# A decode block on one core: w2's rows 16 to 19 loaded in three pieces by partitions, w2's transfer list recut, the output projection's weights in two transfers

## The chip, the cores and the metric

The kernel runs on one core of one Trainium2 chip. The metric is device time in microseconds (us) of one execution, the median of several runs. Before the change it is 139.92 us, the median of three runs from 139.88 to 140.01. One further execution was profiled; rows and durations in this text come from that one.

## The reference

Four sequences of one token each go through attention over a sliding window of a cache, and then through a gated feed-forward layer. Both parts have a layer norm ahead of them and a residual sum behind them. All arrays are bfloat16.

```python
def _A_ref(x, k_cache, v_cache, wq, wo):      # x: 4 x 1 x 1024
    W = min(4096, max(256, Sk // 4))          # Sk = 8192, so W = 2048
    q = (x @ wq).reshape(B, Sq, Hq, Dh).transpose(0, 2, 1, 3)     # 32 heads of 128
    k = jnp.repeat(k_cache[:, :, Sk - W:, :], rep, axis=1)        # 4 kv heads, each for 8 q heads
    v = jnp.repeat(v_cache[:, :, Sk - W:, :], rep, axis=1)
    p = softmax(jnp.einsum("bhqd,bhkd->bhqk", q, k) * Dh ** -0.5)
    o = jnp.einsum("bhqk,bhkd->bhqd", p, v)
    return o.transpose(0, 2, 1, 3).reshape(B, Sq, Hq * Dh) @ wo   # wo: 4096 x 1024

def _B_ref(x, w1, w3, w2):                    # w1, w3: 1024 x 3584; w2: 3584 x 1024
    return (silu(x @ w1) * (x @ w3)) @ w2

h = x + _A_ref(layernorm(x), k_cache, v_cache, wq, wo)
return h + _B_ref(layernorm(h), w1, w3, w2)
```

## The kernel before

There is little arithmetic and much to load: the windows of the two caches, and the five weight matrices, each byte of which is used once. The kernel is one straight program, and the order of instructions on each engine is the order in which they are written.

**The ring of loads.** Every large load goes through one list, `ring`, in the order k, wq, v, wo, w1, w3, w2. (Two of its entries, `kT`, load nothing: they are room for the transposed keys.) An entry takes one of five slots in SBUF, each of 128 partitions by 32 KB (`NSLOT`, `SLOT`). `fill()` walks the list. It issues the transfers of an entry from SP's queue at line 133, one per part of the entry, and it stops at an entry whose slot is not free. An entry's slot is free when every part of the entry five places earlier has been marked by `done()`, which calls `fill()` again. SP itself then waits until the readers of that slot have finished. All these transfers share SP's one hardware queue (q1 in the profile).

**wo.** `wo_v` puts 32 rows of `wo` on each partition, as four groups g (one for each kv head) of eight rows. Eight rows of 1024 bfloat16 numbers are 16 KB. `wo_` has four parts of one group each, 2 MB a transfer, and `pair` puts two of them into one entry. The loop at line 434 runs over g, then over eight rows t and four column blocks c. It reads `get("wo", g)` and calls `done("wo", g)` after each group. The slot of groups 0 and 1 is taken over by the second half of w3, and that of groups 2 and 3 by the first entry of w2.

**w2.** `w2_v` puts 28 rows of w2 on each partition, 2 KB each. `W2B = [16, 8, 2, 2]` cuts them into four transfers. The first, of 16 rows (4 MB), fills an entry by itself. The other three, of 8, 2 and 2 rows, share the last entry of the ring. Its slot comes free when the first half of w1 has been used. The loop at line 491 goes through the parts in order. For each row it has four matmuls, one per column block, with `hg_T` as the weights and 256 numbers of that row as the moving operand; 28 rows make 112 matmuls, accumulated in `y2_ps`. Then `res` adds the residual (line 501), and two small stores, on SP's and ACT's queues (lines 503 and 504), end the kernel.

**Order at the end.** PE goes through `y_ps` (wo), the second layer norm, `gu_ps` for w1 and then for w3, a transpose of the gated product by VectorE, and `y_ps` for w2. (The profile gives wo's and w2's accumulators the same name; the line tells them apart, 434 and 491.)

Of the kernel before, what the change touches and what calls it, by code (L numbers as in the profile page):

```python
# [17 lines left out]
NSLOT = 5  # L18
SLOT = 16384
NEG = -1.0e30  # L20


@with_exitstack
def kernel(
# [20 lines left out]
    nc = tc.nc  # L45

    B, _, D = A_x.shape
    Hkv, Sk, Dh = A_k_cache.shape[1], A_k_cache.shape[2], A_k_cache.shape[3]
# [11 lines left out]
    DQ = D // C  # L60
# [10 lines left out]
    T = REP  # L71
# [4 lines left out]
    wo_v = A_wo.rearrange("(g p t) n -> p g (t n)", g=Hkv, t=T)  # L76
# [16 lines left out]
    def pair(parts):  # L93
        return [parts[0:2], parts[2:4]]
# [3 lines left out]
        for name, cache in (("k", A_k_cache), ("v", A_v_cache))  # L98
    )
    kT_ = pair([("kT", b, [JR, P], None) for b in range(B)])  # L100
    wo_ = pair([("wo", g, [1, T * D], wo_v[:, g : g + 1, :]) for g in range(Hkv)])

    def four_rows(name, view, n):
        return [[(name, i, [4, n], view[:, 4 * i : 4 * i + 4, :])] for i in range(KC // 4)]

    wq_ = four_rows("wq", wq_v, NQ)
    ring = k_ + wq_[:1] + kT_ + wq_[1:] + v_ + wo_ + four_rows("w1", w1_v, F) + four_rows("w3", w3_v, F)
    W2B = [16, 8, 2, 2]
    w2_ = []
    f0 = 0  # L110
    for i, n in enumerate(W2B):
        w2_.append(("w2", i, [n, D], w2_v[:, f0 : f0 + n, :]))
# [6 lines left out]
    def fill():  # L119

        while len(taken) < len(ring):
            n = len(taken) - NSLOT
            if n >= 0 and not all((name, i) in used for name, i, _, _ in ring[n]):
                break
            parts = ring[len(taken)]
            slot = stream.tile([P, SLOT], BF16, tag="slot", name="s_" + parts[0][0])
            o = 0
            for name, i, shape, src in parts:
                dst = slot[:, o : o + int(np.prod(shape))]
                o += int(np.prod(shape))  # L130
                view = dst.rearrange("p (a b) -> p a b", a=shape[0])
                if src is not None:
                    nc.sync.dma_start(out=dst if name in ("k", "v") else view, in_=src)  # L133
                views[(name, i)] = view
            taken.append(slot)

    def get(name, i):
        return views[(name, i)]

    def done(name, i):  # L140
        used.add((name, i))
        fill()
# [5 lines left out]
    nc.vector.memset(x_nat[:], 0.0)  # L148
    nc.scalar.dma_start(out=x_nat[::S, :], in_=x_flat.rearrange("b (c n) -> c b n", c=C))
    fill()  # L150

    ident = const.tile([P, P], BF16)
# [8 lines left out]
        out=t32[:], in_=ident[:].rearrange("p (q h) -> p h q", q=C), axis=AX.X, op=ALU.add  # L161
# [4 lines left out]
    for q in range(C):  # L166
# [3 lines left out]
        out=negm[:], in_=t32[:].rearrange("p (g r) -> p g r", g=Hkv), axis=AX.X, op=ALU.add  # L170
    )
    nc.vector.tensor_scalar(
        out=negm[:], in0=negm[:], scalar1=-1.0, scalar2=-NEG, op0=ALU.add, op1=ALU.mult
    )
    jmask = const.tile([P, JM, 1], FP32)
    nc.vector.tensor_reduce(
        out=jmask[:, :, 0], in_=ident[:].rearrange("p (j h) -> p j h", j=JM), axis=AX.X, op=ALU.add
# [6 lines left out]
    for l in range(2):  # L184
        nc.gpsimd.tensor_copy(
            out=strip[:, l, B - 1 :].rearrange("p (c x) -> p c x", c=C)[:, :, : B * Hkv].rearrange(
                "p c (g b) -> p c g b", b=B
            )[:, :, :, 0],
            in_=t32[:].rearrange("p (g c l) -> p l c g", g=Hkv, c=C)[:, l],
# [62 lines left out]
    for i in range(KC // 4):  # L252
        w = get("wq", i)
        for kk in range(4):
            kc = 4 * i + kk
            for hf in range(2):
                for c in range(C):
                    o = (2 * c + hf) * HALF * Dh
# [3 lines left out]
                        rhs=w[:, kk, o : o + HALF * Dh],  # L262
# [15 lines left out]
    for b in range(B):  # L278
        nc.vector.tensor_copy(  # L279
            out=Qm[:, b].rearrange("p (g y) -> p g y", y=QW)[:, :, :REP],  # L280
            in_=qT_ps[:, :, :, S * b].rearrange("p r g -> p g r"),
# [125 lines left out]
    for l in range(2):  # L407
        for b in range(B):
# [3 lines left out]
                rhs=om[:, b],  # L412
# [10 lines left out]
        out=oP[:, :, :, ::S],  # L423
        in_=oX[:, :, : Hkv * B].rearrange("p t (g b) -> p g t b", b=B),
# [2 lines left out]

    y_ps = ps.tile([P, DQ], FP32, tag="kt0")
    for g in range(Hkv):
        w = get("wo", g)  # L430
        for t in range(T):
            for c in range(C):
                o = t * D + c * DQ
                nc.tensor.matmul(  # L434
                    y_ps[R * c : R * c + R, :],
                    lhsT=oP[:, g, t, :],
                    rhs=w[:, 0, o : o + DQ],
                    start=(g == 0 and t == 0),
                    stop=(g == Hkv - 1 and t == T - 1),
                    tile_position=(0, R * c),  # L440
                )
        done("wo", g)
    h1 = act.tile([P, DQ], FP32)
    nc.vector.tensor_tensor(out=h1[:], in0=y_ps[:], in1=x_nat[:], op=ALU.add)
    h_T = act.tile([P, KC, R], FP32)
# [40 lines left out]
    fc = 0  # L486
    for i, n in enumerate(W2B):
        w = get("w2", i)
        for ff in range(n):
            for c in range(C):  # L490
# [3 lines left out]
                    rhs=w[:, ff, c * DQ : (c + 1) * DQ],  # L494
# [40 lines left out]
```

## Time and profile before

| | |
|---|---|
| median of three runs | 139.92 us |
| the profiled execution | 140.13 us |
| its span, first to last instruction | 138.3 us |
| mean granted TensorE clock | 0.781 of full speed |
| busy: PE, PEld, DVE, ACT, POOL | 80.2, 47.5, 52.9, 42.7, 4.2 us |
| bytes read from HBM | 55.58 MB, 402 GB/s over the span |
| wo's transfers, 2 MB each: issue to landing | median 25.5 us, longest 29.9 us |
| w2's transfers: 16 rows; 8 rows; 2 rows (twice) | 28.0; 25.7; 27.0 us (median) from issue to landing |

PE is TensorE's matmuls, PEld its weight loads, DVE VectorE, ACT ScalarE, POOL GpSimd, and SP the engine that only issues transfers here. "L133" is line 133 of the kernel. A name such as `s_w` is a slot of the ring, with the buffer's number left out; `s_w` stands for w1, w3 and w2 alike. Engine rows are summed over the whole span; they overlap, so their sum is more than the span. In the page's row of 40 slices a digit is the busy share of a slice in tenths, with 9 for 90% or more. A chain of waits is followed backwards from the last instruction: at each step to whatever released it, or to the instruction ahead of it on its engine. The time of one execution is somewhat longer than its span, since it also holds what lies before the first instruction and behind the last.

### The profile page before, as it was taken

How to read it: one execution, taken by the hardware profiler on the slowest of the kernel's cores; microseconds unless marked ns; L12 is line 12 of the kernel's file. 1: busy time of each engine (PE TensorE's matmuls, PEld its weight loads, DVE VectorE, ACT ScalarE, POOL GpSimd, SP SyncE). 2: the span in 40 equal slices, each digit the busy share in tenths (PEclk: the TensorE clock that was granted, in tenths of full speed). 3: DMA queues.
4: the chain of work that ended last, by engine and by line, in shares of the span. 5: the costliest groups of instructions: out<-in, count | busy, mean ns of one | idle time of the engine just before them, and what ended most of it. 6: DMA issues, size and time to landing. Idle time of an engine off the chain costs nothing.

```text
span 138.3 us, 2012 instructions
## 1 busy us (share of the span) xinstructions
PE 80.2 (58%) x866; PEld 47.5 (34%) x868; DVE 52.9 (38%) x97; ACT 42.7 (31%) x57; POOL 4.2 (3%) x18
## 2 busy tenths in 40 slices
PE   0029898921903889328918998659539901703780
PEld 0029887820301322014304434537324400202550
DVE  3036676520000235177087197540330298350001
ACT  3005988850000325998807900000040200000000
POOL 7400000000000000000000000000000000000000
PEclk9999999998555799975797799965865896555555
DMA  4999999999989999999999999999999999999930
GB/s 152 399 423 431 431 436 455 455 441 398 445 384 426 441 417 417 450 407 431 450 400 431 433 469 431 394 448 448 419 398 448 456 411 430 445 407 398 406 148 2
DMA packets 3217, 55.72 MB, mean 403 GB/s; under 512 B 360, under 2 KB 392, under 8 KB 648
## 3 DMA queue, kind: packets, MB, share of 16 engines
q1 hardware_dynamic: 3178, 55.58, 94.4%
q8 instruction: 7, 0.11, 0.3%
q10 hardware_dynamic: 30, 0.01, 0.0%
q14 instruction: 2, 0.02, 0.0%
HBM read 55.58 MB, written 0.01 MB: 402 GB/s over the span
## 4 chain that ended last, share of the span: by engine, by line
DMA 49%; PE 27%; DVE 13%; ACT 4%; SPq 3%; issue 2%; DVEq 0%
DMA s_wq<-in_A_wq_dram 29%; DMA s_w<-in_B_w_dram 20%; PE o_ps L369 10%; PE y_ps L434 5%; ACT P L334 4%; PE sc_ps L294 3%; DVE PT L346 3%; SPq L133 3%; PE gu_ps L458 2%; PE q_ps L259 2%; DVE om L386 2%; DVE od L378 2%; PE on_ps L409 1%; PE tot_ps L355 1%; PE nm_ps L323 1%
## 5 line engine op out<-in xcount | busy, mean ns | idle before, releaser
L334 ACT ACTIVATE P<-sc_ps,bias 128x512 bf16<-128x512 f32 x16 | 19.7, 1417 | 9.6 <-DVE bias L331 9.6
L241 PE MATMUL kt_ps<-ident,s_k 128*128 128x128 bf16 x256 | 17.3, 228 | 1.3 <-ACT s_kT L245 1.0
L369 PE MATMUL o_ps<-s_v,PT 128*128 128x512 bf16 x62 | 17.5, 439 | 0.3 <-issue 0.2
L241 PEld LDWEIGHTS <-s_k 128*128 128x128 bf16 x256 | 16.3, 103 | 2.3 <-issue 1.7
L245 ACT COPY s_kT<-kt_ps 128x1024 bf16<-128x1024 bf16 x16 | 15.7, 1012 | 2.5 <-PE kt_ps L241 2.5
L458 PE MATMUL gu_ps<-s_w,n_T 128*32 128x448 bf16 x128 | 10.7, 513 | 8.8 <-DMA s_w<-in_B_w_dram 6.8
L259 PE MATMUL q_ps<-s_wq,n_T 128*32 128x512 bf16 x64 | 7.0, 615 | 11.8 <-DMA s_wq<-in_A_wq_dram 11.8
L243 DVE COPY s_kT<-kt_ps 128x1024 bf16<-128x1024 bf16 x16 | 11.1, 693 | 5.8 <-PE kt_ps L241 5.8
L491 PE MATMUL y_ps<-s_w,hg_T 128*32 128x256 bf16 x112 | 6.6, 418 | 8.0 <-DMA s_w<-in_B_w_dram 8.0
L369 PEld LDWEIGHTS <-PT 128*128 128x128 bf16 x64 | 7.2, 117 | 9.2 <-issue 4.4
L346 DVE STREAM_TRANSPOSE PT<-P 128x2048 bf16<-128x2048 bf16 x4 | 9.2, 2303 | 2.7 <-ACT P L334 2.7
L208 ACT ACTIVATE rstd<-rstd,eps_t 128x4 f32<-128x4 f32 x2 | 0.6, 297 | 29.5 <-DVE rstd L207 29.5
L458 PEld LDWEIGHTS <-n_T 128*32 128x32 bf16 x128 | 4.7, 131 | 14.1 <-issue 11.6
L294 PE MATMUL sc_ps<-s_kT,Qm 128*32 128x512 bf16 x64 | 8.5, 603 | 0.4 <-DVE Qm L279 0.4
L491 PEld LDWEIGHTS <-hg_T 128*32 128x32 bf16 x112 | 4.9, 142 | 10.0 <-issue 5.9
L259 PEld LDWEIGHTS <-n_T 128*32 128x32 bf16 x64 | 2.7, 137 | 15.6 <-issue 15.5
L269 DVE CAST q_sb<-q_ps 128x512 bf16<-128x512 f32 x1 | 0.7, 692 | 18.3 <-PE q_ps L259 18.3
L198 PE MATMUL sums_ps<-both,ones_f 128*128 128x64 f32 x4 | 1.1, 373 | 11.2 <-DVE both L196 11.2
L434 PE MATMUL y_ps<-s_wo,oP 128*32 128x256 bf16 x128 | 6.5, 397 | 1.7 <-DVE oP L422 1.7
L378 DVE SCALAR_TENSOR_TENSOR od<-o_ps,rinv,jmask 128x512 f32<-128x512 f32 x4 | 3.0, 751 | 8.4 <-PE o_ps L369 8.3
L270 ACT CAST q_sb<-q_ps 128x512 bf16<-128x512 f32 x1 | 0.6, 585 | 17.8 <-PE q_ps L259 17.8
L310 PE MATMUL mx_ps<-ident_f,rmax 128*1 128x128 f32 x8 | 1.7, 302 | 7.4 <-DVE rmax L308 7.4
(68 smaller groups left out, 64.7 us busy)
## 6 DMA issues: line engine op xcount, KB each, us to landing
s_w<-in_B_w_dram SPq DMA_DIRECT2D x4, 3584.0 KB, 21.2
s_k<-in_A_k_cache_dram SPq DMA_DIRECT2D x4, 2048.0 KB, 16.1
s_wq<-in_A_wq_dram SPq DMA_DIRECT2D x2, 4096.0 KB, 35.3
s_v<-in_A_v_cache_dram SPq DMA_DIRECT2D x4, 2048.0 KB, 25.1
s_wo<-in_A_wo_dram SPq DMA_DIRECT2D x4, 2048.0 KB, 25.5
s_w<-in_B_w_dram SPq DMA_DIRECT2D x1, 4096.0 KB, 28.0
s_w<-in_B_w_dram SPq DMA_DIRECT2D x1, 2048.0 KB, 25.7
s_w<-in_B_w_dram SPq DMA_DIRECT2D x2, 512.0 KB, 27.0
```

The lines of the kernel that those rows point to most:

```text
L241: nc.tensor.transpose(out=kt_ps[:, jj], in_=k[:, jb * JB + jj, :], identity=ident[:])
L243: nc.vector.tensor_copy(out=kT[:, jb * JB : (jb + 1) * JB], in_=kt_ps[:])
L245: nc.scalar.copy(out=kT[:, jb * JB : (jb + 1) * JB], in_=kt_ps[:])
L259: nc.tensor.matmul(q_ps[hf][R * c : R * c + R], lhsT=xn_T[:, kc, :], rhs=w[:, kk, o : o + HALF * Dh], start=(kc == 0), stop=(kc == KC - 1) ...
L294: nc.tensor.matmul(sc_ps[b][R * q : R * q + R], lhsT=Qm[:, b, g * R : (g + 1) * R], rhs=v[:, g, q], start=(g == 0), stop=(g == Hkv - 1), t ...
L334: nc.scalar.activation(out=P4[:, :, :, g], in_=sc_ps[b][:].rearrange("p (j i) -> p j i", i=L5), func=ACT.Exp, bias=bias[:, g : g + 1], sca ...
L346: nc.vector.transpose(out=PT[:].rearrange("p j h -> p (j h)"), in_=stage.pop(("P4", b))[:].rearrange("p j i g -> p (j i g)"),)
L369: nc.tensor.matmul(o_ps[:], lhsT=PT[:, i * JM : (i + 1) * JM, :].rearrange("p j h -> p (j h)"), rhs=v[:, i * JM : (i + 1) * JM, :], start= ...
L378: nc.vector.scalar_tensor_tensor(out=od[:], in0=o_ps[:], scalar=rinv[:, 0:1], in1=jmask[:].to_broadcast([P, JM, Dh]), op0=ALU.mult, op1=AL ...
L434: nc.tensor.matmul(y_ps[R * c : R * c + R, :], lhsT=oP[:, g, t, :], rhs=w[:, 0, o : o + DQ], start=(g == 0 and t == 0), stop=(g == Hkv - 1 ...
L458: nc.tensor.matmul(out_ps[hf][R * c : R * c + R], lhsT=hn_T[:, kc, :], rhs=w[:, kk, o : o + FH], start=(kc == 0), stop=(kc == KC - 1), til ...
L491: nc.tensor.matmul(y2_ps[R * c : R * c + R, :], lhsT=hg_T[:, fc, :], rhs=w[:, ff, c * DQ : (c + 1) * DQ], start=(fc == 0), stop=(fc == FC ...
```

## The change

It has three parts.

1. The four transfers of wo become two, each of two groups (4 MB). The projection's loop reads half of a transfer for each group, and marks a transfer as done after its second group.
2. w2 is cut into 16, 4, 4, 2 and 2 rows instead of 16, 8, 2 and 2. The last four parts share the last entry of the ring.
3. The second of these parts (rows 16 to 19 of each partition, 8 KB) is loaded by three transfers one after another on SP's queue, for partitions 0 to 111, 112 to 119 and 120 to 127.

The bytes loaded, the matmuls and their order are the same.

```diff
+PIECES = [0, 112, 120, 128]
...
-    wo_ = pair([("wo", g, [1, T * D], wo_v[:, g : g + 1, :]) for g in range(Hkv)])
+    wo_ = [[("wo", i, [2, T * D], wo_v[:, 2 * i : 2 * i + 2, :])] for i in range(Hkv // 2)]
...
-    W2B = [16, 8, 2, 2]
+    W2B = [16, 4, 4, 2, 2]
...
-                if src is not None:
+                if (name, i) == ("w2", 1):
+                    for p0, p1 in zip(PIECES[:-1], PIECES[1:]):
+                        nc.sync.dma_start(out=view[p0:p1], in_=src[p0:p1])
+                elif src is not None:
                     nc.sync.dma_start(out=dst if name in ("k", "v") else view, in_=src)
...
     for g in range(Hkv):
-        w = get("wo", g)
+        w = get("wo", g // 2)
...
-                    rhs=w[:, 0, o : o + DQ],
+                    rhs=w[:, g % 2, o : o + DQ],
...
-        done("wo", g)
+        if g % 2 == 1:
+            done("wo", g // 2)
```

## The prediction

> **What bounds the kernel now.** I read the page's DMA row first, then the chain of waits from its end, then the timeline of the last 30 us, then the last 3 us in quarter-microsecond windows.
>
> ```profile
> span 138.3 us, 2012 instructions
> DMA  4999999999989999999999999999999999999930
> q1 hardware_dynamic: 3178, 55.58, 94.4%
> ```
> The loads never pause: 55.58 MB go through SP's one queue, whose packets fill 94.4% of sixteen engines' span. The end of the chain of waits (start, length, what) says the same:
>
> ```profile
> 106.04 0.33 SPq L133
> 106.37 0.05 issue
> 106.42 0.43 SPq L133
> 106.84 0.05 issue
> 106.89 27.36 DMA s_w<-in_B_w_dram
> 134.26 0.04 issue
> 134.30 0.64 PE y_ps L491 x8
> 134.94 0.02 issue
> 134.97 0.42 DVE res L501
> ```
> The last w2 transfer is issued at 106.89 and lands 27.36 us later, because everything issued before it is ahead of it. After it come 0.64 us of matmuls, 0.42 us of `res` and the store. The timeline (start, length, engine, line) shows that PE has caught up by then:
>
> ```profile
> 126.88 3.61 PE L491 MATMUL y_ps<-s_w,hg_T 128*32 128x256 bf16 x64 [6.53 <-DMA s_w<-in_B_w_dram]
> ...
> 131.77 2.33 PE L491 MATMUL y_ps<-s_w,hg_T 128*32 128x256 bf16 x40 [1.28 <-DMA s_w<-in_B_w_dram]
> ...
> 134.30 0.62 PE L491 MATMUL y_ps<-s_w,hg_T 128*32 128x256 bf16 x8 [0.20 <-DMA s_w<-in_B_w_dram]
> ```
> So the last landing sets the time. The windows (stretch, its length, busy us of PE, PEld, DVE, ACT, POOL, clock, DMA share, GB/s) show that the sixteen engines do not finish together:
>
> ```profile
> 131.50:131.75 0.25, 0.00 (x0) 0.00 (x0) 0.00 (x0) 0.00 (x0) 0.00 (x0) 0.50 1.02 410
> 131.75:132.00 0.25, 0.23 (x8) 0.20 (x11) 0.00 (x0) 0.00 (x0) 0.00 (x0) 0.50 0.66 262
> 132.00:132.25 0.25, 0.25 (x12) 0.22 (x8) 0.00 (x0) 0.00 (x0) 0.00 (x0) 0.50 0.57 229
> 132.50:132.75 0.25, 0.25 (x12) 0.22 (x8) 0.00 (x0) 0.00 (x0) 0.00 (x0) 0.50 0.44 180
> 133.50:133.75 0.25, 0.25 (x12) 0.22 (x5) 0.00 (x0) 0.00 (x0) 0.00 (x0) 0.50 0.21 82
> 133.75:134.00 0.25, 0.25 (x8) 0.05 (x1) 0.00 (x0) 0.00 (x0) 0.00 (x0) 0.50 0.00 0
> ```
> At 131.75 all are busy; by 132.5 the share is 0.44, seven of sixteen; by 133.8 none.
>
> The trace's DMA records say which. Each packet has a start, a length and a size, but no engine; yet a packet starts 3 to 4 ns before the one ahead of it on its engine ends, so the records can be strung into sixteen chains. Each chain comes out as 176 data packets and 22 completion packets in SP's order. Their last w2 packets end at: seven between 131.73 and 132.00, then 132.31, 132.61, 133.07, and six between 133.62 and 133.78. The six late chains are those that also carried one of the six 16 KB instruction packets of queue q8 that start between 20.5 and 112.9 us; each put its chain back by some 1.7 us. The chain ending at 133.07 and that at 132.61 carried q14's two packets. The four chains that carried `x_nat` (sixteen rows on ACT's queue) are none of the six. Those four belong to eight chains that ran in step in the first 5 us; all six late ones come from the other eight, which then ran out of step. (For three of the six that half is less sure: between 46 and 80 us an end of theirs falls within 1 ns of one of the first eight's, where strings can be swapped.)
>
> **The change, part by part.** *wo in two transfers.* Two of four SP issues go (0.33 to 0.54 us each). The last wo transfer is issued at 53.2 and the longest takes 29.9 us to land: 83.1. PE's first read is at 92.28 and waits for DVE's `oP`. The slack is 9 us, the bytes are the same, and `fill()` acts after the same groups as before, since a slot is freed only when both its halves are used. Cost 0; without that slack a late landing would move `y_ps` one for one.
>
> *w2 as 16, 4, 4, 2, 2.* SP issues six transfers at the end instead of three: 6 x 0.43 = 2.6 us from 106.04, so to 108.6. Queue q1 still holds over 20 us of work then, which hides it (2.6 - 1.28 = 1.3 us if it did not); behind them on SP is only the store, at 135.42. PE's first matmul on the split part waits for three landings, not one. No row shows a triple wait; a queue step on the chain costs 0.02 to 0.14 us, so two more are 0.04 to 0.28 us. They fall where PE has room: the late chains get through that part some 4.9 us (2.44 + 1.22 + 1.22, for the eight rows behind it) before their end, at 128.6, and PE is on the first 64 matmuls until 130.49. Sixteen matmuls then take 16 x 58 ns (2.33 us for 40) = 0.93 us against 2.44 us between landings, and the last 8 still take 0.64. Nothing is added at the end.
>
> *The three pieces.* Four rows are 8 KB a partition. A 16 KB packet takes 0.609 us start to start, so 8 KB takes 0.305, and 64 KB (eight partitions) 2.44. With 112 partitions over sixteen engines each gets seven packets; the two pieces of eight partitions give, if eight engines share them, two more to these. So eight engines carry 9 x 8 KB and eight carry 7 x 8 KB where all carried 8: +0.305 us and -0.305 us. Completion packets (6 ns each) don't count. If the six late chains lie among the relieved eight, they end at 133.78 - 0.305 = 133.47, and the latest of the loaded eight at 133.07 + 0.305 = 133.38. The last data packet then comes 0.305 us earlier, and landing, matmuls, `res` and store follow as before.
>
> The trace only half supports that placement: few-row transfers do use few engines (`x_nat` four chains, the ACT store two), none of them late, and the six are in one half. [...]
>
> What no row shows is whether eight rows into neighbouring partitions, or 112 dealt by sevens, go at full pace. Lower bound: 0.305 us a piece; in `x_nat`, 512 B packets that overlap on two chains take 27 ns, as those alone do. Upper bound: all eight rows in turn, 2.44 us a piece, 4.88 for both where 0.61 is planned: +4.27 us on the loaded chains, whose latest would end at 137.65, 3.9 us past today's end. I take the lower, by the `x_nat` packets, and keep the upper for the range.
>
> [...]
>
> *Sum.* Profiled run: span 138.3 - 0.3 = 138.0, plus the 1.83 us around it (140.13 - 138.3) is 139.83. That run is 0.21 us over the median of 139.92, so the forecast is **139.62 us**.
>
> **Rivals.**
> 1. *The rows of a piece share one way in.* Four in turn, halfway in powers of two from one to eight, make a piece 1.22 us, and the loaded chains lose 2 x (1.22 - 0.305) = 1.83 us. The usual early chain ends at 132.0 + 0.305 + 1.83 = 134.1, 0.35 us late; the one at 133.38 ends at 135.2, 1.43 us late, if it meets others at all, being 1.1 us behind them. That is 140.27 to 141.35, about 140.8. It decides from where a piece costs 0.2 us more than planned: 133.38 + 2 x 0.2 is today's end. For it: eight adjacent partitions and engines that start together. Against: the early chains have 1.7 us to spare.
> 2. *A late chain is among the loaded eight.* Then 133.78 + 0.305: 140.22. Against: the halves above.
> 3. *The load spreads otherwise* (the pieces on all engines alike): 139.92, nothing changes.
> 4. *The next instruction packet.* It starts at 133.48, when PE is at about matmul 93 of 112, on an engine already idle for 0.4 us or more. Row 23 now lands 2.44 us before the late chains' end plus the 0.48 us from last packet to landing (133.78 to 134.26), at 131.5; 13 matmuls on, at 132.3, PE asks for that packet, 1.2 us sooner, and it could meet q1 packets: 1.1 us more on a chain that is last, 141.0. Against: the idle engine was not one of the six, so its relieved or early end leaves room.
>
> **How the numbers follow.** A measurement tells 0.2%, 0.28 us, from no change. Forecast case: 0.50, of which faster 0.32 and within 0.18 (0.305 us is hardly above 0.28). Rival 1: 0.32, slower 0.29, within 0.03. Rival 2: 0.07, slower 0.06, within 0.01. Rival 3: 0.04. Rival 4: 0.05, slower. The last 0.02 is for a larger gain. Faster 0.34, within 0.26, slower 0.40. The forecast's own range is 139.50 to 139.80; the whole reaches to rival 1's far end: 139.5 to 141.3, leaving out about one in ten for longer pieces.
>
> **What would show it.** Right: the last `y_ps` group starts near 134.0; late chains 0.3 us earlier and chains with `x_nat` 0.3 us later; `wo` landed before 84; DMA share at 132.5 above 0.44 and zero by 133.5. Rival 1: 8 KB packets of 0.5 us or more just before 131, with the `x_nat` chains last. Rival 2: the six late ones at 134.1. Rival 4: a q8 packet that overlaps w2 packets on a chain that ends last. I am wrong if the split part lands later than PE's 64th matmul, or if w2's rate falls below 400 GB/s before 131.

## The result, and the profile after

The changed kernel takes 144.08 us, the median of five runs from 143.94 to 144.34. The kernel before took 139.99 us beside it (five runs, 139.88 to 140.01). The ratio is 1.0296, with a 95% interval from 1.0282 to 1.0309. The change makes the kernel slower by 4.1 us; the forecast was 139.62, in a range from 139.5 to 141.3.

The profiled execution took 143.94 us. From its page, the span and the DMA rows, in 40 slices of 3.55 us:

```profile
span 142.1 us, 2013 instructions
...
DMA  4999999999999999999999999999999999999940
GB/s 148 427 415 434 424 438 489 443 411 406 424 406 429 438 434 411 420 429 438 436 424 411 454 453 412 433 436 420 433 428 428 452 429 415 406 242 189 344 180 2
```

The DMA engines are as busy as before, but from the 36th slice on they move 242, 189 and 344 GB/s, where mostly 400 to 450 is usual. A busy share says that packets are in flight; only the rate beside it says how fast. The end of the chain of waits (start, length, what) has the same form as before; line numbers are those of the changed kernel, whose L497 and L507 are L491 and L501 of the kernel before:

```profile
110.37 27.53 DMA s_w<-in_B_w_dram
137.91 0.04 issue
137.95 0.64 PE y_ps L497 x7
138.59 0.02 issue
138.62 0.42 DVE res L507
```

The last landing is still what PE waits for. It comes at 137.91 instead of 134.26, and these 3.65 us are nearly all of the difference between the two spans (142.1 - 138.3 = 3.8). To see where they arise, take the tail in windows of 2 us (stretch, length, busy us of PE, PEld, DVE, ACT and POOL, granted clock, DMA share, GB/s). First the kernel before, then the changed one:

```profile
124.00:126.00 2.00, 0.00 (x0) 0.00 (x0) 0.00 (x0) 0.00 (x0) 0.00 (x0) 0.50 0.77 328
126.00:128.00 2.00, 1.12 (x24) 0.98 (x27) 0.00 (x0) 0.00 (x0) 0.00 (x0) 0.50 0.96 410
128.00:130.00 2.00, 2.00 (x44) 1.75 (x40) 0.00 (x0) 0.00 (x0) 0.00 (x0) 0.50 1.02 432
130.00:132.00 2.00, 0.71 (x20) 0.35 (x13) 0.00 (x0) 0.00 (x0) 0.00 (x0) 0.50 0.91 367
```

```profile
124.00:126.00 2.00, 0.00 (x0) 0.00 (x0) 0.00 (x0) 0.00 (x0) 0.00 (x0) 0.50 0.96 254
126.00:128.00 2.00, 0.00 (x0) 0.00 (x0) 0.00 (x0) 0.00 (x0) 0.00 (x0) 0.50 0.90 193
128.00:130.00 2.00, 1.80 (x36) 1.53 (x39) 0.00 (x0) 0.00 (x0) 0.00 (x0) 0.50 1.06 176
130.00:132.00 2.00, 1.55 (x36) 1.06 (x28) 0.00 (x0) 0.00 (x0) 0.00 (x0) 0.71 0.96 221
132.00:134.00 2.00, 0.62 (x16) 0.45 (x17) 0.00 (x0) 0.00 (x0) 0.00 (x0) 1.00 0.94 350
```

Between 126 and 132 all sixteen engines together move 176 to 221 GB/s, half of what they did, and yet their share is 0.90 to 1.06. The clock of TensorE is no part of this; PE waits. In the DMA records, with their one duration per packet, 193 of the 256 packets of 8 KB take over 0.34 us (the usual one takes 0.31), the longest 1.11. Only 128 of the 256 belong to the pieces, so at least 65 packets of the four-row transfer behind them are slow too. Packets of the 16-row transfer *ahead* of the pieces are hit as well: on engines that are still at it, their 32 KB packets take up to 2.2 us instead of 1.22. From 133 on packets have their usual length again, and the last three transfers land 1.25 us apart, as transfers of 32 KB an engine at full pace do. Summed over all of w2's packets and divided by sixteen, the excess is 3.9 us an engine, which is the whole loss.

On PE one sees the same (timeline: start, length, engine, line, the idle time before it):

```profile
128.20 3.35 PE L497 MATMUL y_ps<-s_w,hg_T 128*32 128x256 bf16 x64 [8.40 <-DMA s_w<-in_B_w_dram]
133.20 0.62 PE L497 MATMUL y_ps<-s_w,hg_T 128*32 128x256 bf16 x16 [1.65 <-DMA s_w<-in_B_w_dram]
135.46 1.05 PE L497 MATMUL y_ps<-s_w,hg_T 128*32 128x256 bf16 x16 [1.64 <-DMA s_w<-in_B_w_dram]
136.71 0.62 PE L497 MATMUL y_ps<-s_w,hg_T 128*32 128x256 bf16 x8 [0.21 <-DMA s_w<-in_B_w_dram]
137.95 0.62 PE L497 MATMUL y_ps<-s_w,hg_T 128*32 128x256 bf16 x8 [0.62 <-DMA s_w<-in_B_w_dram]
```

The first 64 matmuls, on the transfer ahead of the pieces, already start 1.3 us later than before (126.88), and the split part is ready 1.65 us after they are done, at 133.20, where the forecast had PE still at work when it came. That, and a rate of some 200 GB/s before 131, are the two signs that the prediction named for being wrong.

### The profile page after: what moved, and what is told of

It is laid out like the page before. It is cut to its first block, busy times and chain, and to the rows that moved or that the text cites. A ratio compares the mean times of both kernels' runs of the same rounds, so it can differ in the third digit from the quotient of the medians.

```text
span 142.1 us, 2013 instructions
## 1 busy us (share of the span) xinstructions
PE 83.2 (59%) x866; PEld 49.1 (35%) x868; DVE 52.8 (37%) x97; ACT 42.8 (30%) x57; POOL 4.2 (3%) x18
## 4 chain that ended last, share of the span: by engine, by line
DMA 47%; PE 28%; DVE 13%; ACT 4%; SPq 3%; issue 2%; DVEq 0%
DMA s_wq<-in_A_wq_dram 28%; DMA s_w<-in_B_w_dram 19%; PE o_ps L374 10%; PE y_ps L439 5%; ACT P L339 4%; PE sc_ps L299 3%; DVE PT L351 3%; SPq L138 3%; PE gu_ps L464 2%; PE q_ps L264 2%; DVE om L391 2%; DVE od L383 2%; PE tot_ps L360 1%; PE nm_ps L328 1%; PE on_ps L414 1%
## 5 line engine op out<-in xcount | busy, mean ns | idle before, releaser
L246 PE MATMUL kt_ps<-ident,s_k 128*128 128x128 bf16 x256 | 18.4, 237 | 0.9
L374 PE MATMUL o_ps<-s_v,PT 128*128 128x512 bf16 x62 | 18.7, 463 | 0.3 <-issue 0.2
L246 PEld LDWEIGHTS <-s_k 128*128 128x128 bf16 x256 | 17.5, 109 | 1.8 <-issue 1.6
L464 PE MATMUL gu_ps<-s_w,n_T 128*32 128x448 bf16 x128 | 10.2, 496 | 6.4 <-DMA s_w<-in_B_w_dram 4.5
L497 PE MATMUL y_ps<-s_w,hg_T 128*32 128x256 bf16 x112 | 6.3, 383 | 12.5 <-DMA s_w<-in_B_w_dram 12.5
L497 PEld LDWEIGHTS <-hg_T 128*32 128x32 bf16 x112 | 4.2, 128 | 14.9 <-issue 8.9
L507 DVE TENSOR_TENSOR res<-y_ps,h 128x256 bf16<-128x256 f32 x1 | 0.4, 424 | 16.2 <-PE y_ps L497 16.2
```

Source lines behind the costliest of these rows:

```text
L246: nc.tensor.transpose(out=kt_ps[:, jj], in_=k[:, jb * JB + jj, :], identity=ident[:])
L374: nc.tensor.matmul(o_ps[:], lhsT=PT[:, i * JM : (i + 1) * JM, :].rearrange("p j h -> p (j h)"), rhs=v[:, i * JM : (i + 1) * JM, :], start= ...
L464: nc.tensor.matmul(out_ps[hf][R * c : R * c + R], lhsT=hn_T[:, kc, :], rhs=w[:, kk, o : o + FH], start=(kc == 0), stop=(kc == KC - 1), til ...
L497: nc.tensor.matmul(y2_ps[R * c : R * c + R, :], lhsT=hg_T[:, fc, :], rhs=w[:, ff, c * DQ : (c + 1) * DQ], start=(fc == 0), stop=(fc == FC ...
```

## The experiments

The theory after this reading, called P, was a supposition of the author's: a packet is slow while another engine writes to the same small group of partitions, which the pieces bring about and transfers of 128 partitions do not. The DMA records name neither the engine nor the partitions of a packet, so no run shows this itself; the runs show which pieces are slow, and by how much. Rivals were the recut itself, the eight-row pieces alone, reads from memory, and a cost that exists only at the tail.

**The change without its pieces**

```diff
-PIECES = [0, 112, 120, 128]
+PIECES = [0, 128]
```

> The change without its pieces: wo in two transfers and w2 as 16, 4, 4, 2, 2 stay, the four rows are one transfer of 128 partitions. Theory P (the pieces cost it all: packets that reach partitions in another way than 16 engines by eights slow each other): 139.7 to 140.2 us, the same as before, and the 8 KB packets take 0.31 us. Rival R (smaller packets and two more transfers in the queue, or the wo merge, cost part): 141 us or more with whole transfers too.

Measured: 139.90 us against 140.09 before, ratio 0.9992 (0.9983 to 1.0002). Its windows:

```profile
126.00:128.00 2.00, 1.18 (x24) 1.03 (x27) 0.00 (x0) 0.00 (x0) 0.00 (x0) 0.50 1.02 426
128.00:130.00 2.00, 2.00 (x47) 1.70 (x41) 0.00 (x0) 0.00 (x0) 0.00 (x0) 0.50 1.01 418
```

The rate stays at 418 to 426 GB/s with packets of 8 KB, all between 0.309 and 0.322 us. The wo merge and the recut cost nothing; the pieces cost all of it. This is the base for what follows.

**112 and 16 partitions**

```diff
-PIECES = [0, 112, 120, 128]
+PIECES = [0, 112, 128]
```

> The four rows in two pieces, 112 and 16 partitions. Theory P1 (the 112 piece, dealt by sevens, is most of the cost: in the changed kernel it took 3.9 us between its landing and the one before where seven packets need 2.1): 142 to 144 us. Rival Q (the two pieces of eight partitions, on eight engines, are the cost): 140 to 140.5 us, since neither is there.

Measured: 143.95 us, ratio 1.028 (1.026 to 1.0301), as slow as the change. Eight-row pieces are not needed for the loss.

**The 112 piece by itself**, beside whole transfers. In this and the later runs with repeated rows, the last slot's unused quarter takes rows a second time, and nothing reads them. Here `ROWS = [slice(0, 112)]`:

```diff
                 if (name, i) == ("w2", 1):
-                    for p0, p1 in zip(PIECES[:-1], PIECES[1:]):
-                        nc.sync.dma_start(out=view[p0:p1], in_=src[p0:p1])
+                    nc.sync.dma_start(out=view, in_=src)
+                    spare = slot[:, 12 * D : 16 * D].rearrange("p (a b) -> p a b", a=4)
+                    for rows in ROWS:
+                        nc.sync.dma_start(out=spare[rows], in_=src[rows])
```

> Whole transfers, and behind the four-row one a transfer that repeats partitions 0 to 111 into the unused part of the slot: the 112 piece by itself. It adds seven packets of 8 KB on each engine, 2.1 us at full pace: 142.0 us if the 112 piece runs at full pace (rival Q, the eight-partition pieces alone are slow). Theory P: its packets take 0.5 us or more and slow those of late engines: 143 to 145 us.

Measured: 145.44 us, ratio 1.0385 (1.0344 to 1.0426): 5.5 us over the base, where 2.1 would be full pace. The 112 piece is slow on its own, and takes 3.4 us too much. The rate, in windows of this run:

```profile
128.00:130.00 2.00, 2.00 (x48) 1.72 (x37) 0.00 (x0) 0.00 (x0) 0.00 (x0) 0.50 0.98 221
130.00:132.00 2.00, 1.10 (x24) 0.57 (x17) 0.00 (x0) 0.00 (x0) 0.00 (x0) 0.76 1.05 242
132.00:134.00 2.00, 0.00 (x0) 0.00 (x0) 0.00 (x0) 0.00 (x0) 0.00 (x0) 1.00 0.97 225
```

**The two pieces of eight adjacent partitions by themselves** (`ROWS = [slice(112, 120), slice(120, 128)]`)

> Whole transfers, and behind the four-row one two more transfers of eight adjacent partitions each (112 to 119, 120 to 127), which repeat part of its load into an unused part of the slot: 16 KB more on each of eight engines, 0.61 us if at full pace. Rival Q (pieces of eight adjacent partitions slow each other and their neighbours): 140.8 to 142 us. P1 (only the 112 piece hurts): 139.9 to 140.2, as the engines that carry them have 0.7 us or more to spare.

Measured: 142.12 us, ratio 1.0149 (1.0129 to 1.0169), 2.2 us over the base for 128 KB.

**The same pieces with partitions spread** (`ROWS = [slice(0, 32, 4), slice(32, 64, 4)]`)

> As the run with adjacent partitions, but the two repeated pieces hold partitions 0, 4, .. 28 and 32, 36, .. 60. The same bytes on the same number of engines. If nearness of the partitions is what slows a piece: 139.8 to 140.2 us here and clearly more with adjacent ones. If any transfer on eight engines costs the same: equal times in both.

Measured: 140.39 us, ratio 1.0026 (1.0014 to 1.0038), 0.5 us over the base, a little more than expected. The same bytes on as many engines; only the partitions differ. Windows with the adjacent pieces, then with the spread ones:

```profile
126.00:128.00 2.00, 1.26 (x25) 1.05 (x28) 0.00 (x0) 0.00 (x0) 0.00 (x0) 0.50 1.13 324
128.00:130.00 2.00, 2.00 (x45) 1.69 (x37) 0.00 (x0) 0.00 (x0) 0.00 (x0) 0.50 0.96 238
```

```profile
126.00:128.00 2.00, 1.12 (x24) 0.94 (x27) 0.00 (x0) 0.00 (x0) 0.00 (x0) 0.50 0.98 410
128.00:130.00 2.00, 2.00 (x44) 1.69 (x40) 0.00 (x0) 0.00 (x0) 0.00 (x0) 0.50 1.00 416
```

238 GB/s against 416. Of the 8 KB packets, the longest is 0.92 us with adjacent partitions and 0.32 with spread ones. Eight rows can go at full pace, and do so here, with the partitions four apart.

**Reads or writes**: the pieces' sources and destinations taken apart. First the adjacent rows of w2 into spread partitions, then the spread rows into adjacent partitions (`for to, of in ROWS: ... dma_start(out=spare[to], in_=src[of])`).

> The two repeated pieces with source and destination taken apart: they read the adjacent rows (those of partitions 112 to 127) and write them to partitions 0, 4, .. 60. [...] Rival U (reading adjacent rows of w2 from memory on several engines at once is slow): as with adjacent pieces, 141.8 to 142.4.

> The counterpart: the pieces read the rows of partitions 0, 4, .. 60 and write them to the adjacent partitions 112 to 127. Theory P: 141.8 to 142.4 us with 8 KB packets of up to 0.9 us. Rival U: 140.2 to 140.6.

Measured: 140.20 us, ratio 1.0012 (0.9999 to 1.0025), and 142.19, ratio 1.0148 (1.0119 to 1.0178). For these pieces the partitions written decide; which rows are read does not matter. The 112 piece and the halves of 64 were not taken apart in this way.

**Two halves of 64**

```diff
-PIECES = [0, 112, 120, 128]
+PIECES = [0, 64, 128]
```

> The change with the four rows in two halves of 64 partitions, sixteen engines each with four packets. [...] Rival T (dealing by sevens, with a size that is no power of two, is the trouble): 139.8 to 140.3.

Measured: 144.54 us, ratio 1.0321 (1.0245 to 1.0396). Powers of two are no better than sevens, so rival T is out. The median of the 8 KB packets is 0.59 us, nearly twice 0.31, and the time is 4.5 us over before. Four packets an engine for each half, at 0.59 instead of 0.31, are an estimate of 8 x 0.28 = 2.2 us. In the windows:

```profile
126.00:128.00 2.00, 0.00 (x0) 0.00 (x0) 0.00 (x0) 0.00 (x0) 0.00 (x0) 0.50 0.80 147
128.00:130.00 2.00, 1.30 (x28) 1.13 (x31) 0.00 (x0) 0.00 (x0) 0.00 (x0) 0.50 1.03 217
130.00:132.00 2.00, 2.00 (x44) 1.60 (x36) 0.00 (x0) 0.00 (x0) 0.00 (x0) 0.50 1.00 221
```

217 and 221 are half the usual rate. The estimate of 2.2 us leaves out two things. While some engines are already at the halves, 32 KB packets of those still at the transfer before take up to 2.5 us. And 194 of the 256 packets of 8 KB take over 0.34 us, though only 128 belong to the halves, so at least 66 of the transfer behind are slow as well. At 220 GB/s the 1 MB of the halves is an estimate of 4.8 us, yet the rate is down in all of these 6 us; what accounts for the rest, no run shows.

**Spread, but in the other half** (`ROWS = [slice(64, 96, 4), slice(96, 128, 4)]`)

> [...] Rival S (only crowding of neighbouring partitions counts, where an engine writes does not): as with the low spread pieces, 140.2 to 140.5, all packets 0.31 us.

Measured: 141.70 us, ratio 1.0118 (1.0086 to 1.015). So it isn't only crowding within the piece (rival S): these pieces are spread as widely as the low ones, 1.8 us over the base instead of 0.5. Packets go up to 0.63 us, and 116 of them are over 0.34 us, though the two pieces hold only sixteen. What sets these partitions apart from 0, 4, .. 60, no run shows.

**Spread, shifted by four partitions** (`ROWS = [slice(4, 36, 4)]`, one piece)

> [...]

Measured: 140.52 us, ratio 1.0034 (1.0023 to 1.0045). That is 0.6 us over the base for one piece, where two low spread pieces cost 0.5. 91 packets of 264 take over 0.34 us, the longest 0.54, though the piece holds only eight: neighbours are disturbed. In windows of 1 us:

```profile
126.00:127.00 1.00, 0.14 (x4) 0.13 (x7) 0.00 (x0) 0.00 (x0) 0.00 (x0) 0.50 1.02 426
127.00:128.00 1.00, 1.00 (x24) 0.83 (x20) 0.00 (x0) 0.00 (x0) 0.00 (x0) 0.50 1.04 328
128.00:129.00 1.00, 1.00 (x28) 0.83 (x24) 0.00 (x0) 0.00 (x0) 0.00 (x0) 0.50 0.99 352
129.00:130.00 1.00, 1.00 (x24) 0.85 (x20) 0.00 (x0) 0.00 (x0) 0.00 (x0) 0.50 0.94 352
130.00:131.00 1.00, 1.00 (x28) 0.85 (x17) 0.00 (x0) 0.00 (x0) 0.00 (x0) 0.50 1.02 418
```

A piece of 0.3 us lowers the rate for some 2.5 us. The disturbance outlasts the piece; why is open.

**The pieces in the middle of the stream**

```diff
-                if (name, i) == ("w2", 1):
+                if (name, i) == ("w3", 0):
```

> The pieces moved from the tail to the middle of the stream: w2's four rows whole, but the first half of w3 (four rows of 7 KB on each partition, 3.5 times the bytes) in pieces of 112, 8 and 8 partitions. Theory P (a piece loses bandwidth wherever it stands, in proportion to its bytes): the 4.1 us of the change times 3.5 makes 14 us, so 150 to 155 us. Rival V (it costs only at the tail, where nothing behind it can fill idle engines): 139.8 to 142 us.

Measured: 153.91 us, ratio 1.0985 (1.0954 to 1.1017): 13.8 us, 3.4 times the change's loss for 3.5 times its bytes. It is lost bandwidth, at the tail and in mid-stream, and rival V is out. Packets of 28 KB, usually 1.07 us, take up to 4.49 us here. Its page has the hole at the 27th to 32nd slice (of 3.8 us), followed by the full rate:

```profile
GB/s 138 434 431 427 423 487 418 410 414 457 410 423 418 444 418 436 414 423 438 431 425 436 460 397 453 385 249 246 287 143 98 204 415 454 440 408 380 390 104 2
```

**A try at a faster version**, on the kernel before:

```diff
-    W2B = [16, 8, 2, 2]
+    W2B = [16, 8, 2, 1, 1]
```

> A try at a faster version, on the kernel before: w2 as 16, 8, 2, 1, 1 rows. After the last landing PE has 4 matmuls instead of 8, which saves some 0.1 to 0.2 us of 0.64, if 2 KB packets keep the pace: 139.8 to 140.0 us. If they don't, the last two rows land 0.1 to 0.4 us later: 140.1 to 140.4.

Measured: 139.83 us against 139.96, ratio 0.9994 (0.9985 to 1.0004). The last group of matmuls is 4 instead of 8 and takes 0.41 us, but the gain can't be told from none. No version here beats the kernel before clearly.

## Why the prediction was wrong

**The step that failed** is "I take the lower, by the `x_nat` packets": it priced the pieces as if they ran at full pace, 0.305 us for each piece of eight rows and nothing extra for the 112. `x_nat`'s packets of 512 B go to partitions eight apart, a few at a time; they could not show what eight rows of 8 KB in neighbouring partitions do. In the change the pieces lose 3.65 us by the landing times.

**The piece that was not priced.** The step named the 112 partitions dealt by sevens, but its upper bound and rival 1 put a cost only on the two eight-row pieces. The 112 piece holds seven eighths of the bytes and, by the runs with repeated rows, makes most of the loss: 3.4 us too much by itself, against some 1.7 us for the eight-row pieces (2.2 over the base with adjacent partitions, 0.5 with spread ones). The two don't add up to the change's 4.1 us, as they are measured beside whole transfers.

**Rival 1** had the direction, but the wrong reach. It let a slow piece delay only the engines that carry it, and so let 1.7 us of slack absorb most of it on the usual early chains. The runs show late engines and other transfers disturbed too: 32 KB packets of 2.2 us ahead of the pieces, and slow 8 KB packets in the transfer behind them. The far bound of that step, 3.9 us past the old end, would have held the landing (3.65 us late), though added to 139.92 it makes 143.8, just short of the 144.08 measured. That it comes so near is luck, as it was worked out for the two small pieces alone. Cutting the range at rival 1 left it out.

**The placement** was half wrong as well. The forecast put all six late chains in the relieved eight, and its 0.305 us rests on that; no run shows that placement. The run with low spread pieces shows who is loaded: the signals of the four-row transfer land at 127.31 to 129.33, and those of the first repeated piece, each 0.3 us behind its engine's own, at 127.63, 127.68, 127.70, 127.72, 127.74, 128.53, 128.71 and 129.23. The last one belongs to the engine that was at 128.91, one of the six late ones (128.91 to 129.33). So in that run one late chain is among the loaded eight, which is rival 2. If the kernel before loads its engines alike, which no record shows, it would have gone from about 133.62 to 133.93 and ended 0.15 us after today's end, and the expected gain was not there even at full pace. The prediction had noted that, for three of the six, chains could have been swapped.

**What held.** wo and the recut at 0 (ratio 0.9992). The last landing sets the end, and all after it follows unchanged: 0.64 us of matmuls and 0.42 of `res` in both. Rival 4 did not happen: the last three transfers land at an even 1.25 us. Rival 3 is out, since the pieces load eight engines alone (the eight signals above).

**What slows a packet** no run shows. Rival 1 supposed that the rows of a piece share one way in, and theory P that engines meet at the same small group of partitions; the records have only the times. Packets of 8 KB take up to 0.92 us with adjacent partitions, and 1.08 when the spread rows are written to them, mostly 0.55 to 0.64 with halves of 64, and 0.31 with partitions 0, 4, .. 60. In the runs with high spread and with shifted pieces, more packets were slow than the pieces hold (116 against 16, 91 against 8). How the engines deal a transfer's rows among them is not seen either.

## What to carry to other kernels

On a queue that is bound by DMA, load with transfers of 128 partitions, and don't balance engines by cutting a transfer along partitions: 64 and 64, 112 and 16, and 112, 8 and 8 all about halved the rate of the whole core while they ran, and cost some 4 us for 1 MB. If a few rows must be loaded apart, time the choice of partitions: for 128 KB, 0, 4, .. 60 cost 0.5 us here, 64, 68, .. 124 cost 1.8, and 112 to 127 cost 2.2. And check the GB/s row: the busy share alone looks full (0.90 to 1.06 at 176 to 221 GB/s). When no row of a profile shows an operation's price, the range has to reach to the far bound, above all where it would disturb work that is not its own.

## What had not been expected of the hardware

A slow transfer slowed the one *ahead* of it: while some engines had finished the 16-row transfer and gone on to the pieces, packets of those still at it took up to 2.2 us instead of 1.22. And one misplaced piece of 64 KB, 0.3 us of work, lowered the rate to 328 and 352 GB/s for 2.5 us; 0.3 us of slow packets does not explain that, and no run here settles it.
